# Nine-token runs for k and v, a product in four quarters, and more transposes by transfer, in a two-part attention and MLP kernel

## The chip, the cores and the metric

The kernel runs on one core of a Trainium2 chip. A core has a matrix engine (PE, fed by a stream of weight loads, PEld), three engines for elementwise work (DVE, ACT, POOL), a queue engine (SP) and 16 DMA engines shared by the queues of SP (q1) and POOL (q0). Matrix results go to PSUM, from where DVE and ACT copy them. The metric is the device time of one execution in microseconds (us), as the median of several runs.

## The reference

There are 8 batches of 8 heads, 576 tokens and 64 columns a head. All inputs and the output are float32.

```python
kv = np.einsum('bhsd,bhse->bhde', k, v)
out = np.einsum('bhsd,bhde->bhse', q, kv)
rms = np.sqrt(np.mean(out * out, axis=-1, keepdims=True) + 1e-06)
x = (out / rms * g_norm)            # then laid out as (batch, 576 tokens, 512 columns)
theta = x @ w_theta
zr, zi = x * np.cos(theta), x * np.sin(theta)
y = np.einsum('ts,bsd->btd', w_tok_r, zr) + np.einsum('ts,bsd->btd', w_tok_i, zi)
u = x + y
return u + np.maximum(u @ w_ch, 0.0)
```

## The kernel before

**Work and order.** Each batch is cut into tasks for one engine each. A batch has five token tiles: four of 128 tokens (j = 0 to 3) and a tail of 64. A long table, `TURNS`, gives the order in which all tasks of all batches are issued; a letter behind a number puts a copy on another engine (A for ACT, D for DVE), and `r15` means 15 matmuls on constants that keep PE busy. Each engine works its own instructions in that order and waits, in order, for what they need. So a task's place in the table decides what stands behind it when it waits.

**A batch, in tasks.** `load k`, `load v` (SP) and `load q` (POOL). `kv`: the product of k and v per head on PE (L278, L285), summed over 576 tokens, in float32. `ko`: copies of it into `kbd` (L307 on ACT, L309 on DVE), each head twice, in the upper and the lower 64 partitions. `qt`/`qd`: q turned, by PE in batches 0 and 1, by a transposing transfer afterwards (L330). `raw`: q times kv (L344, L353). `sq`, `ss`, `rt`, `x`: square (ACT), sum (DVE), reciprocal root (POOL, L382), scaled x (DVE, L405). `xt`/`xd`: x turned, by PE (L302, tile `xps`) in batches 0 to 4 and by a transfer (L433, tile `xd`) from batch 5 (`XD`). `xo`: its copy, scaled by g (L257 on ACT, L259 on DVE). `th`: x times w_theta (L464, L467). `pt`, `ar`, `ab`, `si`, `co`, `z`: reduction of the angle, sine, cosine, products with x (ACT and DVE). `y`: the token product on PE (L554), the largest piece of work. `um`: u (DVE, L569). `ut`/`ud`: u turned back, by PE (L302, tile `ups`) or, in batches 5 and 6 (`UD`), by a transfer (L596). `v`: u times w_ch (L464, L467). `fin` and `st`: the last sum (DVE, L612, L617) and the store (SP).

**The weights.** At the start POOL's queue loads the theta weights (`wth`) and the imaginary and real token weights (`toki`, `tokr`), SP's the channel weights, which are scaled once (`wc`, L259 on POOL). PE turns the token weights in nine pieces (`wt`, L642, L643), DVE or ACT copies each into `wT` (`wo`, L307, L309). No y can start before them and before the first z.

**How k and v lie.** In batch 0 a partition holds nine consecutive tokens of a head, and a pair of heads fills 128 partitions. In the other batches 128 partitions hold four tokens each of every head, and the last 64 tokens are a second transfer (L206) into a tile whose lower half is padded with zeros. A head pair there takes ten matmuls of 128 rows by 64 columns, five steps of two heads side by side; the four pairs share one accumulator.

```python
    PS_TR, PS_RAW, PS_ACC = ("tr", 2), ("raw", 2), ("acc", 4)
```

There are four accumulators of the kind `acc`: kv, th, y and v take them in turn, and one is free again when its readers are done.

Of the kernel before, what the change touches and what calls it, by code (L numbers as in the profile page):

```python
# [9 lines left out]
FP32 = mybir.dt.float32  # L10
# [19 lines left out]
0 1 8 4 5 6 7 2 18 3 9 10 11 14 15 r15 31 39 32 47 13 16 17 24 25 33 40 34A 48 23 19 20 35 49 41 36  # L30
55 50 42 51 37 52 38A 12 56D 53 54 21 63 71 57 64D 43 72 58 73 65 74 44 r2 137 133 59 45 75 46 60 66
76 138A 134A 61 62 67 77 68 79 89 125 90D 69 70 126 80 91 107 92 108 81D 78 93 98 82 116 117D 94 99
83 95 118 100 129 127 84 85 119 96 86 101 128 87 130 102 120 97 121 88 109 139 141 171 159 122 110
104 123 140 142A 103 124 111 112 105 28 29 26 22 206 27 207 208 30 201 163 135 131 202 113 136 114
106 132D 115 203 204 155 172 160 161 229 173 164 165 156 215 216 162 174 230 166 167 157 147 148 143
168 169 144 158 170 222 145 185 209 210 211 212 149 151 213 186 223D 214 146 150 152 217 231 236 153
243 218 232 237 244 219 154 220 233 205 388 366 377 187 190 175 234 357 188 221 177 192 224 191 176
178 235 225 250 226 251D 238 259 358 227 239 260D 240 193 353 354 514 355 194 356 189 195 252 180
261 196 253 181 262 228 254 245 360 361 241 255 242 263 264 268 362 363 246 256 257 265 266 364 365
247 269D 258 248 359 249 270 286 277 389 271 390 287D 278 288 182 267 391 272 273 183 279 315 367  # L40
289 274 392 275 290 393 291 276 378 311 280 292 293 281 282 379 283 323 312 319 320 430 316 324 284
368 431 294 501 525 502 536 503 504 179 285 369 317 313 318 314 380 505 370 381 321 307 308 325 303
322 326 371 304 305 309 299 300 432 310 382 403 394 433 306 404D 395D 342 301 372 383 396 373 384
397 302 374 434 435 405 347 197 508 509 510 511 406 348 436 437 385 398 407 399 408 438 198 375 386
441 440 439 506 442 295 296 344 400 343 401 513 512 409 376 387 345 402 412 515 526 297 421 422D 298
413 516 410 414 337 423 332 339 349 517 411 415 338 527 416 417 350 528 418 424 419 507 518 529 653
519 425 426 340 530 656 657 658 659 451 542 520 427 428 660 521 420 661D 522 334 537 459 452 662 523
429 543 538 333 335 524 460 453 471 472 473 551 454 539 540 531 461 455 532 552 474 673 684 346 649
650 184 651 652 533 541 456 467 457 468 469 663 534 462 458 535 470 578 327 553 664 328 554 665 579D
463 674 464 560 666 654 465 580 675 555 561D 466 676 556 557 581 558 667 582 677 562 544 563 583 564  # L50
565 685 447 448 329 490 569 545 584 686 566 567 570 585 491 443 449 444 445 546 559 678 687 450 586
446 330 688 571 690 492 668 689 547 691 572 548 669 341 821 810 336 475 679 477 726 573 568 574 727D
670 493 655 589 590 587 588 801 671 797 331 798 832 799 800 494 804 476 575 680 478 681 699 805 806
807 497 728 495 700 549 809 550 808D 496 576 729 682 701 485 692 498 672 730 577 731 480 599 600 591
811 592 593 702 481 486 683 703 822 717 607 601 812 693 705 704 694 594 602 813 814 732 733 823 696
608 603 609 604 605 595 718D 610 734 815 606 824 719 596 597 708 619 735 825 738 802 720 709 706 598
721 695 707 620 615 616 710 621 611 833 826 711 834 697 612 613 623 617 622 722 835 618 836 736 803
737 837 712 698 713 614 625 628 487 816 827 482 714 624 828 817 715 488 626 829 818 483 716 950 629
723 724 838 479 956 872 943 951 952 953 643 767 819 725 847 644 955 820 954D 763 751 764 752 768 769
765 747 748 830 749 638 957 753 831 766 770 873D 754 750 958 839 959 962 848 630 755 960 484 967 855  # L60
489 627 978 944 849 963 756 757 874 850 851 964 631 840 945 946 875 852 639 841 758 961 876 965 947
739 743 740 744 741 968 745 759 842 877 966 742 856 969 853 878 746 970 864D 879 760 640 973 771 761
# [3 lines left out]
898 899 985 904 908 983 896 993D 977 986 889 890 1096 987 900 988 1097 994 891 885 1098 892 909 1107  # L66
1099 995 1108 1018 1001 632 989 996 1109 1110 786 886 913 887 914 888 1100 997 990 1019 998 991 999
1002 1010D 782 915 910 911 1101 1020 783 916 912 1111 992 352 775 1117 637 199 1003 1118 793 937
1102 1021 1022 1023 784 1011 1004 1024 1103 1005 794 499 780 642 1123 917 796 785 648 1104 1025 1012
1119 918 928 923 1026 1013 1120 1006 1014 1105 1007 787 919 1008 924 929 1000 1132D 788 1015 1030  # L70
# [4 lines left out]
1141D 1139 1150 1142 940 1161 1162 935 1151 1152 1074 1163 1143 1164 1084 1144 1085 1069 1075 1146  # L75
# [27 lines left out]
def kernel(  # L103
# [12 lines left out]
    nc = tc.nc  # L116
    B, H, S, D = q.shape
    C = H * D
    P = 128
# [21 lines left out]
    NX, NXE = 7, 4  # L141
    QD = 2

    XD = 5
    UD = (5, 6)

    ZD = 2
# [750 lines left out]
```

## Time and profile before

| | |
|---|---|
| median of the runs shown | 220.69 us (220.33 to 221.16, 3 runs) |
| the profiled execution's own time | 222.68 us |
| its span, first to last instruction | 220.9 us |
| mean granted clock of PE | 0.973 |
| PE busy | 200.5 us, 91% |
| DVE busy | 175.2 us, 79% |
| ACT busy | 132.2 us, 60% |
| POOL busy | 97.3 us, 44% |
| transfers | 70,059 packets, 43.43 MB, mean 197 GB/s |

Busy time counts an engine that is at work. Matmuls overlap, so an instruction's duration on PE is longer than the distance to the next; the distance is what a row of many equal instructions shows. The chain of work that ended last is followed back from the last instruction, at each step to what released it. A wait is put down to the semaphore that came last.

### The profile page before, as it was taken

How to read it: one execution, taken by the hardware profiler on the slowest of the kernel's cores; microseconds unless marked ns; L12 is line 12 of the kernel's file. 1: busy time of each engine (PE TensorE's matmuls, PEld its weight loads, DVE VectorE, ACT ScalarE, POOL GpSimd, SP SyncE). 2: the span in 40 equal slices, each digit the busy share in tenths (PEclk: the TensorE clock that was granted, in tenths of full speed). 3: DMA queues.
4: the chain of work that ended last, by engine and by line, in shares of the span. 5: the costliest groups of instructions: out<-in, count | busy, mean ns of one | idle time of the engine just before them, and what ended most of it. 6: DMA issues, size and time to landing. Idle time of an engine off the chain costs nothing.

```text
span 220.9 us, 5506 instructions
## 1 busy us (share of the span) xinstructions
PE 200.5 (91%) x2177; PEld 137.7 (62%) x2177; DVE 175.2 (79%) x371; ACT 132.2 (60%) x268; POOL 97.3 (44%) x102
## 2 busy tenths in 40 slices
PE   7398699799799999989999999999999999999991
PEld 2275356596465768757578776866587746756850
DVE  4018649627989989897999988999997999999662
ACT  2028479317499249762788854947865888557050
POOL 8225930002953529556649158435724545204000
PEclk9969769999999999999999999999999999999998
DMA  6999999954999999959999976998980776764374
GB/s 229 274 275 238 236 231 234 271 163 27 260 140 209 297 183 306 122 85 258 307 203 289 137 226 137 240 240 225 163 141 12 225 181 166 178 114 117 110 262 154
DMA packets 70059, 43.43 MB, mean 197 GB/s; under 512 B 39570, under 2 KB 63762, under 8 KB 70034
## 3 DMA queue, kind: packets, MB, share of 16 engines
q1 hardware_dynamic: 55602, 35.73, 64.7%
q0 software_dynamic: 14432, 7.36, 25.0%
q8 instruction: 17, 0.28, 0.5%
q14 instruction: 8, 0.07, 0.1%
HBM read 33.06 MB, written 9.44 MB: 192 GB/s over the span
## 4 chain that ended last, share of the span: by engine, by line
PE 60%; DVE 14%; DMA 9%; POOL 8%; ACT 5%; issue 2%; POOLq 0%; DVEq 0%; ACTq 0%
PE y L554 26%; PE v L464 10%; PE th L464 10%; DMA wth<-in_moe_w_theta_dram 9%; POOL rt L382 5%; PE kv L285 5%; DVE arg L486 2%; DVE ss L375 2%; PE ups L302 2%; PE raw L344 2%; DVE x L405 2%; DVE zm L531 2%; PE th L467 2%; PE xps L302 1%; PE v L467 1%
## 5 line engine op out<-in xcount | busy, mean ns | idle before, releaser
L382 POOL TENSOR_TENSOR rt<-ss,mhalf 128x8 f32<-128x8 f32 (+1 forms) x35 | 54.9, 1572 | 81.7 <-DVE ss L375 81.5
L554 PE MATMUL y<-wT,zm 128*128 128x256 f16 (+1 forms) x512 | 76.0, 286 | 1.9 <-DVE zm L531 1.0
L554 PEld LDWEIGHTS <-zm 128*128 128x128 f16 x512 | 47.7, 98 | 17.2 <-DVE zm L531 2.6
L569 DVE SCALAR_TENSOR_TENSOR wn<-y,gcol,xT 128x256 f16<-128x256 f32 (+2 forms) x72 | 32.6, 478 | 8.2 <-PE y L554 7.7
L464 PE MATMUL th<-wth,xT 128*128 128x512 f16 x128 | 34.2, 395 | 2.0 <-DMA wth<-in_moe_w_theta_dram 1.6
L480 ACT ACTIVATE pt<-th 128x512 f32<-128x512 f32 (+1 forms) x40 | 21.8, 550 | 20.7 <-PE th L464 13.1
L464 PE MATMUL v<-wch,wn 128*128 128x512 f16 x128 | 31.6, 379 | 0.0
L486 DVE SCALAR_TENSOR_TENSOR arg<-pt,th 128x512 f32<-128x512 f32 (+1 forms) x40 | 24.8, 627 | 4.2 <-ACT pt L480 4.0
L509 ACT ACTIVATE sc<-arg,quarter 128x512 f16<-128x512 f32 (+1 forms) x40 | 27.0, 675 | 1.2 <-DVE arg L494 1.1
L502 ACT ACTIVATE sc<-arg 128x512 f16<-128x512 f32 (+1 forms) x40 | 23.4, 587 | 6.9 <-DVE arg L486 6.6
L366 ACT ACTIVATE sqb<-raw 128x512 f32<-128x512 f32 x32 | 18.5, 592 | 14.7 <-PE raw L344 13.4
L405 DVE TENSOR_TENSOR x<-raw,rt 128x512 f16<-128x512 f32 x32 | 21.8, 684 | 3.0 <-POOL rt L382 2.6
L375 DVE TENSOR_REDUCE ss<-sqb 128x8 f32<-128x520 f32 x32 | 21.8, 686 | 2.5 <-ACT sqb L366 2.3
L531 DVE TENSOR_TENSOR zm<-x,sc 128x1024 f16<-128x1024 f16 x32 | 21.7, 682 | 0.5 <-ACT sc L509 0.5
L617 DVE SCALAR_TENSOR_TENSOR us<-v,us 128x512 f32<-128x512 f32 (+1 forms) x32 | 19.4, 616 | 2.0 <-PE v L467 0.8
L307 ACT CAST kbd<-kv 64x256 f16<-64x256 f32 (+1 forms) x28 | 9.4, 334 | 19.1 <-PE kv L278 12.4
L464 PEld LDWEIGHTS <-xT 128*128 128x128 f16 x128 | 11.6, 100 | 13.4 <-issue 3.3
L588 ACT ACTIVATE us<-ups 128x512 f32<-128x512 f16 (+1 forms) x32 | 17.0, 541 | 4.1 <-PE ups L302 2.6
L537 POOL DMA_DIRECT2D zt<-zf x24 | 13.6, 574 | 12.4 <-PE v L467 11.1
L464 PEld LDWEIGHTS <-wn 128*128 128x128 f16 x128 | 11.8, 98 | 11.2 <-issue 0.6
L285 PE MATMUL kv<-vt,kt 128*64 128x64 f32 x560 | 18.3, 223 | 0.0
L554 PE MATMUL y<-wT,zt 128*128 128x320 f16 (+1 forms) x64 | 18.3, 286 | 0.0
(78 smaller groups left out, 249.2 us busy)
## 6 DMA issues: line engine op xcount, KB each, us to landing
kt<-in_k_dram SPq DMA_DIRECT2D x7, 1024.0 KB, 9.1
vt<-in_v_dram SPq DMA_DIRECT2D x7, 1024.0 KB, 8.0
out_dram<-us SPq DMA_DIRECT2D x24, 256.0 KB, 3.4
qh<-in_q_dram POOLq DMA_DIRECT2D x7, 512.0 KB, 11.3
out_dram<-vs SPq DMA_DIRECT2D x8, 256.0 KB, 2.3
zm<-in_moe_w_ch_dram SPq DMA_DIRECT2D x1, 1024.0 KB, 12.0
out_dram<-us SPq DMA_DIRECT2D x16, 64.0 KB, 2.1
kt<-in_k_dram SPq DMA_DIRECT2D x7, 128.0 KB, 7.4
```

The costliest lines, as they stand in the source:

```text
L285: nc.tensor.matmul(t[i * D:(i + 1) * D, hp - lo, :], kt[b % NKV][:, 2 * hp + i, j, :], vt[b % NKV][:, 2 * hp + i, j, :], start=(j == 0), s ...
L375: nc.vector.reduce_sum(out=ss[:], in_=sq_sb.pop((b, j))[:], axis=AXX)
L382: nc.gpsimd.tensor_tensor(out=rt[:], in0=ss[:], in1=mhalf[:, 0:h], op=ALU.pow)
L405: nc.vector.tensor_tensor(out=x_pair[b, p][:, :, a * HC:(a + 1) * HC].rearrange("p t (h e) -> p h t e", e=D), in0=r[:].rearrange("p (h t e ...
L464: nc.tensor.matmul(t[:], lhs(kc), w[:, kc, :], start=first, stop=last)
L480: nc.scalar.activation(out=pt[:], in_=th_ps[b, j][:], func=AFT.Copy, bias=MAGIC)
L486: nc.vector.scalar_tensor_tensor(out=arg[:, 0, :], in0=pt_sb.pop((b, j))[:], scalar=MAGIC, in1=th_ps.pop((b, j))[:], op0=ALU.subtract, op1 ...
L502: nc.scalar.activation(out=sc[:, 0, :], in_=arg_sb[b, j][:, 0, :], func=AFT.Sin, bias=0.0, scale=-TURN * SHRINK,)
L509: nc.scalar.activation(out=sc_sb[b, j][:, 1, :], in_=arg_sb.pop((b, j))[:, 1, :], func=AFT.Sin, bias=quarter[:], scale=-TURN * SHRINK,)
L531: nc.vector.tensor_tensor(out=dst, in0=x.unsqueeze(1).broadcast_to((P, 2, w)), in1=sc[:], op=ALU.mult)
L554: nc.tensor.matmul(t[:, 0:hi - lo], s, wT[:, w, lo:hi], start=n == 0, stop=n == len(z) - 1)
L569: nc.vector.scalar_tensor_tensor(out=dst, in0=y_in, scalar=gcol[:, 0:1], in1=x_in, op0=ALU.mult, op1=ALU.add,)
```

## The change

**k and v** now lie in nine-token runs in every batch: one transfer for k and one for v, without the tails and without the padding. A head pair's even head is in the upper 64 partitions and its odd head in the lower.

**The product** (`kv_quad`, task `kq`) handles four heads at a time: 36 matmuls of 64 rows by 64 columns, in the order upper rows and left columns, lower rows and left columns, upper and right, lower and right. The two row halves write two different accumulators, so a batch holds two; both quads of a batch use the same two, except in batch 0, where each has its own.

**The copies** take one accumulator at a time: eight pieces of 64x128 a batch (sixteen of 64x64 in batch 0), each contiguous in `kbd`, whose heads lie in a new order (`slot`).

**Turning.** x is turned by a transfer from batch 3 on (before: 5), u in batches 4, 5 and 6 (before: 5 and 6).

**Order.** The whole table is new. The diff, with the table cut to its first lines:

```diff
 TURNS = """
-0 1 8 4 5 6 7 2 18 3 9 10 11 14 15 r15 31 39 32 47 13 16 17 24 25 33 40 34A 48 23 19 20 35 49 41 36
...
+0 1 7 8 9 10 13 14 12 2 r11 27 3 30A 5 31A 6 28 19 r2 45 37 4 46 29D 17 38 47 18 39 48 40 49 53 61
...
-    XD = 5
-    UD = (5, 6)
+    XD = 3
+    UD = (4, 5, 6)
...
-    kt = [const.tile([P, H, NT, D], FP32, name=f"kt{i}") for i in range(NKV)]
-    vt = [const.tile([P, H, NT, D], FP32, name=f"vt{i}") for i in range(NKV)]
+    kt = [const.tile([P, NHP, S], FP32, name=f"kt{i}") for i in range(NKV)]
+    vt = [const.tile([P, NHP, S], FP32, name=f"vt{i}") for i in range(NKV)]
...
     def pairs_in(eng, dst, src, b, lo, hi):
         eng.dma_start(
-            out=nines(dst)[:, lo:hi, :],
+            out=dst[:, lo:hi, :],
...
-    def heads_in(eng, dst, src, b, hs):
...
-    def tails_in(eng, dst, src, b, hs):
...
-    def pad(eng, i):
...
+    def kv_quad(b, g, banks):
+        if banks is None:
+            banks = [ps.tile([P, NG, D], FP32, tag="acc", bufs=4, name="kv") for r in range(2)]
+        for j in range(NN):
+            js = slice(j * D, (j + 1) * D)
+            for c in range(2):
+                for r in range(2):
+                    at = slice(r * D, (r + 1) * D)
                     nc.tensor.matmul(
+                        banks[r][c * D:(c + 1) * D, g, :], kt[b % NKV][at, 2 * g + c, js],
+                        vt[b % NKV][at, 2 * g + c, js], start=(j == 0), stop=(j == NN - 1),
                     )
+        for r in range(2):
+            kv_ps[b, g, r] = banks[r]
+
+    def slot(h):
+        return 4 * (h % 2) + 2 * (h // 2 % 2) + h // 4
+
+    def kv_out(b, gs, r, i, eng):
+        at = slice(i * D, (i + 1) * D)
+        lo, n = gs[0], len(gs)
+        for c in range(2):
+            src = kv_ps[b, lo, r][c * D:(c + 1) * D, lo:lo + n, :]
+            first = slot(4 * lo + 2 * c + r)
+            copy_out(eng, kbd[b % 2][at, first:first + n, at], src)
...
-    for a, (lo, hi) in enumerate(((0, NH2), (NH2, NH2 + 1), (NH2 + 1, NHP))):
...
+    for a in range(NG):
+        k_got[0, a] = [add(f"load {x}0{'ab'[a]}", "SP",
+                           lambda a=a, t=t, src=src: pairs_in(nc.sync, t[0], src, 0, 2 * a, 2 * a + 2))
+                       for x, t, src in (("k", kt, k), ("v", vt, v))]
         if not a:
+            add("hold s", "SP", lambda: hold_sync(vt[0][0:1, 0, 0:1]), k_got[0, 0][1:])
...
+        k_ = [add(f"load k{b}n", "SP", lambda: pairs_in(nc.sync, kt[b % NKV], k, b, 0, NHP), old),
+              add(f"load v{b}n", "SP", lambda: pairs_in(nc.sync, vt[b % NKV], v, b, 0, NHP), old)]
```

Three places show how the order moves.

POOL at the start; `wn_86` and `wnt_88` are the imaginary token weights, `wn_85` and `wnt_87` the real ones, `wch` the scaled channel weights, `qh_69` q of batch 1. Before:

```order
L224 DMA wn_86<-in_moe_w_tok_i_dram 128x2304
L229 DMA wnt_88<-in_moe_w_tok_i_dram 64x576
L232 DMA wth<-in_moe_w_theta_dram 128x4x512
L224 DMA wn_85<-in_moe_w_tok_r_dram 128x2304
L229 DMA wnt_87<-in_moe_w_tok_r_dram 64x576
L212 DMA qh_69<-in_q_dram 128x8x256
```

Now:

```order
L209 DMA wn_86<-in_moe_w_tok_i_dram 128x2304
L214 DMA wnt_88<-in_moe_w_tok_i_dram 64x576
L217 DMA wth<-in_moe_w_theta_dram 128x4x512
L240 TENSOR_SCALAR wch<-zm_77 128x512
L209 DMA wn_85<-in_moe_w_tok_r_dram 128x2304
L214 DMA wnt_87<-in_moe_w_tok_r_dram 64x576
L240 TENSOR_SCALAR wch<-zm_77 128x512
L197 DMA qh_69<-in_q_dram 128x8x256
```

Two scalings of the channel weights, which wait for these weights, have moved ahead: one in front of the real token weights, one in front of q of batch 1.

ACT from its first `pt` (L480, now L462) in batch 0 through sine and cosine (L502, L509; now L484, L491); `wT` is a copy of turned token weights, `xT` of turned x. Before:

```order
L480 ACTIVATE pt<-th 128x512
L257 ACTIVATE xT_82<-xps,gcol 128x4x128 x2
L480 ACTIVATE pt<-th 128x512
L502 ACTIVATE sc<-arg 128x512
L480 ACTIVATE pt<-th 128x256
L509 ACTIVATE sc<-arg,quarter 128x512
L502 ACTIVATE sc<-arg 128x512
L480 ACTIVATE pt<-th 128x512
L307 COPY wT<-wps 128x576
L509 ACTIVATE sc<-arg,quarter 128x512
L502 ACTIVATE sc<-arg 128x256
L480 ACTIVATE pt<-th 128x512
```

Now:

```order
L462 ACTIVATE pt<-th 128x512 x2
L484 ACTIVATE sc<-arg 128x512
L491 ACTIVATE sc<-arg,quarter 128x512
L462 ACTIVATE pt<-th 128x512
L484 ACTIVATE sc<-arg 128x512
L491 ACTIVATE sc<-arg,quarter 128x512
L289 COPY wT<-wps 128x576
L462 ACTIVATE pt<-th 128x256
L462 ACTIVATE pt<-th 128x512
```

The two copies of x have left the chain. Of four weight copies between the first pt and the last cosine, one is left; the others are on DVE (before, three more follow the rows shown).

SP around x of batch 3, now turned by transfers (`xd`), between stores (`out`), q of batches 4 and 5 (`qD`) and k, v of batch 5:

```order
L190 DMA kt_65<-in_k_dram 128x4x576
L312 DMA_TRANSPOSE qD<-qe_72 128x2x128
L607 DMA out_dram<-us 128x512
L415 DMA_TRANSPOSE xd<-x 128x8x128
L312 DMA_TRANSPOSE qD<-qh_69 128x8x128
L415 DMA_TRANSPOSE xd<-x 128x2x128
L607 DMA out_dram<-us 128x512 x2
L190 DMA vt_67<-in_v_dram 128x4x576
L415 DMA_TRANSPOSE xd<-x 128x8x128
```

Before, no `xd` stands there; each k and v of batch 5 was a pair of transfers, and nothing of x was ahead of v.

More of the change, by code (lines that the diff above doesn't have):

```diff
@@ L717 @@
         ko = {}
[L718 to L726 removed]
+        first = None
+        for g in range(NG):
+            own = b == 0 or not g
+            t = add(f"kq {b} {g}", "PE",
+                    lambda b=b, g=g: kv_quad(b, g, [kv_ps[b, 0, r] for r in range(2)] if g and b else None),
+                    [*k_got[b, g], None if own else first], [PS_ACC, PS_ACC] if own else [])
+            if own:
+                first = t
+            last["kv", b] = t
+            if b and not g:
+                continue
+            gs = [g] if b == 0 else [0, 1]
+            outs = []
+            for r in range(2):
+                for i in range(2):
+                    outs.append(add(f"ko{len(gs)} {b} {g}{r}{i}", "DVE" if r else "ACT",
+                                    lambda e, b=b, gs=gs, r=r, i=i: kv_out(b, gs, r, i, e),
+                                    [t, *of("raw", b - 2), *(outs[-1:] if i else [])],
+                                    alt=("ACT", "DVE")))
             first.readers = outs
[L728 to L730 removed]
+            ko.update({x: outs for x in gs})
         ko[2] = ko[0] + ko[1]
```

141 lines of the change are left out of this document (34 added, 107 removed), and 32 rows, old and new, of the table TURNS.

## The prediction

> **What bounds the kernel now.** I read the page first, then the busy time in four stretches, then the chain of work that ended last, and only then the rows of the parts that the change touches.
>
> ```profile
> span 220.9 us, 5506 instructions
> ...
> core 0: us, PE busy (x) PEld busy (x) DVE busy (x) ACT busy (x) POOL busy (x), PEclk, DMA share, GB/s
> 0.00:42.00 42.00, 31.29 (x321) 19.81 (x322) 21.18 (x56) 21.11 (x46) 17.89 (x28) 0.88 1.13 247
> 42.00:110.00 68.00, 63.18 (x804) 44.91 (x801) 56.88 (x114) 40.55 (x83) 34.27 (x29) 1.00 0.97 198
> 110.00:210.00 100.00, 99.96 (x1015) 69.73 (x1009) 92.56 (x196) 67.38 (x134) 45.09 (x46) 1.00 0.80 173
> 210.00:220.90 10.90, 6.09 (x50) 3.27 (x48) 4.55 (x9) 3.15 (x6) 0.00 (x0) 0.93 0.58 205
> ```
>
> Three regimes. To 42 us, transfers and then a chain over ACT and DVE keep PE from its main work, and the clock is at 0.88. From 42 to 110, PE (63 of 68) and DVE (57 of 68) alternate. From 110 to 210, PE is without a gap and DVE is 92.6% busy: whatever leaves PE there is worth time only until DVE fills up.
>
> ```profile
> 5.42 20.46 DMA wth<-in_moe_w_theta_dram
> 25.92 1.86 PE th L464 x4
> ...
> 41.35 0.58 PE y L554 x3
> ...
> 137.34 0.45 PE raw L344 x8
> 137.79 0.86 PE v L464 x4
> 138.65 2.52 PE kv L285 x80
> ```
>
> The chain says the same in order: the theta weights land at 25.9, the token product (y) runs steadily only from 41.35, and later PE follows PE. It also gives PE's real prices: 0.86/4 = 215 ns for a 512-column matmul, 0.45/8 = 56 ns for a 128-column one, 2.52 us for the k-v product of a batch.
>
> **The k-v product.** Before, a batch has 40 matmuls of 128 rows by 64 columns (two instructions each in the trace, being fp32), two column halves side by side. Now it has 72 of 64 by 64, four quarters side by side, hence 144 instructions.
>
> ```profile
> L285 PE MATMUL kv<-vt,kt 128*64 128x64 f32 x560 | 18.3, 223 | 0.0
> ...
> 6.21 1.26 PE L278 MATMUL kv<-vt,kt 64*64 64x64 f32 x36
> 47.49 2.55 PE L285 MATMUL kv<-vt,kt 128*64 128x64 f32 x80
> 19.43 0.32 PE L353 MATMUL raw<-kbd,qT 128*64 128x64 f16 x8
> ...
> L353 PE MATMUL raw<-kbd,qT 128*64 128x64 f16 x16 | 0.6, 201 | 0.1
> ```
>
> Without the last instruction's own 0.22 us, 80 in 2.55 are 29.5 ns apart, and 36 of batch 0, which already work in two diagonal quarters, are (1.26-0.22)/35 = 29.7 ns apart. Half the rows make a matmul no quicker, so the spacing is that of two units, each taking one per 59 ns. With four units it would be 14.7 ns: 144 x 14.7 = 2.1 us against 2.36, a gain of 0.2 us a batch. With no overlap of the two row halves it stays at 29.5: 4.25 us, a loss of 1.9 a batch. The two-byte row lets me choose: eight instructions in 0.32 us with 0.20 for the last are (0.32-0.20)/7 = 17 ns apart, so instructions can be issued nearly that densely. I take the gain. The page "TensorE: Matmul & The Clock Gate" of the Trainium skill (section "Wait — 56ns, not 53.3ns?") says that start-to-start never falls below about 25 ns; by it a batch would take an estimated 3.6 us, and the whole forecast would stand near 225 us. The trace's 17 ns speaks against this floor where halves work side by side.
>
> **Copies out of the product.** Four of 64x256 a batch become eight of 64x128, and in batch 0 eight of 64x128 become sixteen of 64x64.
>
> ```profile
> L307 ACT CAST kbd<-kv 64x256 f16<-64x256 f32 x20 | 7.3, 364 | 6.5 <-PE kv L285 6.3
> L309 DVE CAST kbd<-kv 64x256 f16<-64x256 f32 x8 | 3.4, 421 | 3.6 <-ACT kbd L307 3.4
> L307 ACT CAST kbd<-kv 64x128 f16<-64x128 f32 x8 | 2.1, 259 | 12.5 <-PE kv L278 12.4
> L569 DVE SCALAR_TENSOR_TENSOR wn<-y,gcol,xT 128x256 f16<-128x256 f32 x40 | 18.6, 478 | 3.4 <-PE y L554 3.1
> L569 DVE SCALAR_TENSOR_TENSOR wn<-y,gcol,xT 128x320 f16<-128x320 f32 x24 | 12.8, 546 | 4.9 <-PE y L554 4.6
> L569 DVE SCALAR_TENSOR_TENSOR wn<-y,gcol,xT 128x64 f16<-128x64 f32 x8 | 2.2, 275 | 0.0
> L259 DVE TENSOR_SCALAR xT<-xps,gcol 128x512 f16<-128x512 f16 x10 | 4.6, 474 | 0.1
> L259 DVE TENSOR_SCALAR xT<-xd,gcol 128x512 f16<-128x512 f16 x5 | 1.7, 343 | 0.0
> ```
>
> On ACT the half-size copy is 259 against 364 ns. DVE has no such row: it lies between its 64-column piece (275) and the full copy (421); ACT's ratio gives 300. In batches 1 to 7 DVE has 24 such copies instead of 8 large ones: 7.2 - 3.4 = +3.8 us, of which batches 4 to 7 have 14 x 0.30 - 6 x 0.42 = +1.7. ACT goes from 20 x 0.364 to 32 x 0.259, +1.0. The product now holds two of the four accumulators until all eight copies are done, where it held one; y, th and v need the rest. I cost that at nothing, since PE has the other two, and keep 0.3 us a batch (one copy's length) as the upper end.
>
> **x by transfers in batches 3 and 4, u in 4.** PE loses 2 x 18 + 16 = 52 transposes of 56 ns: 2.9 us, all after 110. ACT keeps a copy for each. DVE cuts u's 320-column pieces in two (4 x (0.478 + 0.275 - 0.546) = +0.8 us) and reads x from a cheaper place (343 instead of 474 ns); over batches 3 to 7 its share of these copies changes from 2 full-size from PSUM, 5 from transfers and 3 half-size ones (about 0.3 us each) to 8 full ones from transfers, about -0.9. Six x and four u transfers join SP's queue.
>
> ```profile
> 8.98 7.05 SPq L206 DMA_DIRECT2D kt<-in_k_dram  x1
> 16.08 5.44 SPq L200 DMA_DIRECT2D vt<-in_v_dram  x1
> 157.85 1.28 SPq L433 DMA_TRANSPOSE xd<-x  x1
> 184.14 1.28 SPq L596 DMA_TRANSPOSE ud<-wn  x1
> ...
> SPq L433 <- DVE x L405: 17.7, 3, 8.9
> ...
> xd<-x SPq DMA_TRANSPOSE x9, 3.2
> ud<-wn SPq DMA_TRANSPOSE x8, 2.5
> ```
>
> Each holds SP for about 1.3 us: +13 us on a queue with room for it, while 14 tail loads leave; two of the many-piece loads alone held SP for 12.5 us at the start. SP now also has q's first transfer of batch 2 ahead of k and v of batches 2 and 3; it waits there for q, but these k are not asked for before 60 us: nothing. The wait added is ACT's and DVE's for a landing, 3.2 us after issue, behind whatever SP waits for first (up to 8.9 us for x). Queued behind a waiting transfer are stores and the next k, v; who waits for it is theta of that batch, and then PE. The new order puts x's transfers of batch 3 right behind the producer, well ahead of th, so I cost the wait at nothing; rival four prices the other case.
>
> **The start.** Three things move. SP holds back the second half of k, v until the first v has landed. POOL issues the real token weights only behind its first scaling of the channel weights. ACT does one of the nine weight copies inside the theta chain instead of four, and no x copy there after the first theta.
>
> ```profile
> 27.82 0.60 ACT L480 ACTIVATE pt<-th 128x512 f32<-128x512 f32 x1 [2.65 <-PE th L464]
> 39.85 0.72 ACT L509 ACTIVATE sc<-arg,quarter 128x512 f16<-128x512 f32 x1
> ...
> L307 ACT COPY wT<-wps 128x576 f16<-128x576 f16 x6 | 3.6, 634 | 0.2 <-PE wps L643 0.2
> L257 ACT ACTIVATE xT<-xps,gcol 128x512 f16<-128x512 f16 x10 | 6.7, 685 | 0.8 <-PE xps L302 0.8
> ...
> 6.19 0.62 POOL L224 DMA_DIRECT2D wn<-in_moe_w_tok_r_dram x1
> 19.46 2.97 POOL L259 TENSOR_SCALAR wch<-zm 128x512 f16<-128x512 f32 x2 [1.88 <-DMA zm<-in_moe_w_ch_dram]
> ...
> wn<-in_moe_w_tok_r_dram POOLq DMA_DIRECT2D x1, 576.0 KB, 22.6
> qh<-in_q_dram POOLq DMA_DIRECT2D x7, 512.0 KB, 11.3
> ```
>
> From the first pt (27.82) to the end of the last cosine (40.57) ACT is what y waits for. Leaving that stretch: 3 x 0.634 + 2 x 0.685 = 3.3 us. Against it: the real token weights now land at 6.19+22.6 = 28.8. After the change they are issued after the first scaling, 19.46+1.5+0.6 = 21.6; with the 11.3 us of a similar load on that queue, 32.9. PE asks for them behind five thetas, at 25.9 + 4 x 0.86 + 0.45 = 29.8, and ACT behind seven activations, about 31.3. So between nothing and about 2 us is lost, and 3.3 us is the gain's upper end. I take **-2.0**, bounds -3.3 and +1.
>
> **The sum**, against the profiled execution's own 222.68 us (span 220.9 and 1.8 around it; the median of the runs, 220.69, is 2.0 below). Start: -2.0. Between 42 and 110: PE -0.6 for three products, DVE +2.1 for three batches of copies, in a stretch where DVE has 11 us free: 0, with 3 either way because the order of a chain over five engines is new. From 110: PE could lose 2.9 + 5 x 0.21 = 3.95; DVE gains 1.7 + 0.8 - 0.9 = 1.6 and would stand at 94.2 in 96 us, 98%. It has not shown that over a whole stretch, so I take **-2.5** (94.2 in 97.5, 96.6%), bounds -3.95 and 0. Tail: the same instructions, 0. Together -4.5: 218.2 in a profiled execution, **216.2 us** as a median. With the bounds of each term that are likely together, 214 to 219 for this case.
>
> **The rivals.** A measurement of this kernel tells about 0.5% (1.1 us) from no change: 219.6 to 221.8 is "same".
> 1. *Forecast*, 216.2: chance 0.45.
> 2. *The middle stretch shortens too.* Fewer k, v pieces free SP and the transfers, which are at 0.97 of 16 engines there, and the order closes gaps: the other 3 us and the rest of the late gain, about 212. For it: PE is 5 us idle there. Against: DVE's copies. Chance 0.13.
> 3. *DVE becomes the bound.* The late gain is lost (+2.5) and the middle pays most of its DVE copies (+1.8): 220.5. For it: 92.6 of 100 already. Against: ACT is 67 of 100 and took part of the copies. Chance 0.17.
> 4. *Slower: the quarters do not run four abreast.* At 29.5 ns a batch's product takes 4.25 us, +1.9 x 7 = 13 us, and the credited 0.7 is gone: 230. Three of the batches lie where PE is 4.8 us idle; with half of that as cover, 227. It outweighs the gains once a batch's 144 instructions take more than 2.36 + (4.5+0.7)/7 = 3.1 us. For it: no row shows more than two units at once. Against: the 17 ns row, and separate accumulators for the two row halves, on which nothing in the trace bears. The page "TensorEngine Tiling (Array Packing)" of the Trainium skill (section "Gotcha 1: PSUM Pressure") says that row tiles cannot use one PSUM bank at the same time; the change keeps to that, and no run here shows what a breach costs. Chance 0.14.
> 5. *The new order waits somewhere*: the token weights stall ACT's whole chain at the start, or SP's queue holds x of batch 3 or 4 (one 8.9 us wait at that place). +6 us on the forecast: 222.5. Chance 0.11.
>
> **Chances.** Faster by over 0.5%: cases 1 and 2, 0.58. Within 0.5%: 0.17. Slower by over 0.5%: cases 4 and 5, 0.25. The range leaves out about half of case 2 and most of case 4: 211.0 to 225.5.
>
> **What would show it.** Right: the block of 144 instructions in 2.1 to 2.5 us; y steady by about 39.5 us; DVE at 95 to 97% in the PE-bound stretch; ten more transfers with PE still without gaps. Wrong: the block near 3.6 or 4.2 us; ACT waiting for the real token weights; PE waiting for x behind a transfer in batches 3 and 4; DVE at 99% with PE waiting for z or for accumulators.

## The result, and the profile after

The changed kernel takes 233.0 us (median of 4 runs, 230.6 to 233.8) against 220.9 (4 runs, 220.3 to 221.5) of the kernel before on the same chip: a ratio of 1.053, 95% interval 1.045 to 1.061. That is 12 us slower, above the upper end of the range. Some of the kernels below show two speeds up to 3% apart; ratios compare undisturbed runs with undisturbed runs, so a median and a ratio can differ by a per cent.

The page of the changed kernel, and its busy time in the stretches that the prediction used:

```profile
span 232.0 us, 6323 instructions
PE 197.2 (85%) x2574; PEld 134.3 (58%) x2574; DVE 181.1 (78%) x398; ACT 133.3 (57%) x279; POOL 96.2 (41%) x100
q8 instruction: 20, 0.33, 0.6%
...
core 0: us, PE busy (x) PEld busy (x) DVE busy (x) ACT busy (x) POOL busy (x), PEclk, DMA share, GB/s
0.00:42.00 42.00, 27.42 (x299) 16.58 (x300) 21.77 (x57) 17.20 (x40) 19.70 (x29) 0.81 1.15 244
42.00:110.00 68.00, 59.69 (x1018) 43.90 (x1016) 55.12 (x121) 37.95 (x82) 29.56 (x26) 0.97 0.87 195
110.00:210.00 100.00, 93.48 (x1134) 62.82 (x1132) 91.55 (x200) 71.23 (x146) 44.83 (x41) 1.00 0.83 181
```

Where PE had no gap before (99.96 of 100 us), it now idles 6.5 us, and between 42 and 110 us another 3.5 more than before. DVE is not fuller: 91.55 of 100 against 92.56.

PE's granted clock fell too, which the prediction did not price: to a mean of 0.81 before 42 us (0.88 before the change) and 0.97 from there to 110 (1.00). Between 100 and 110 us it was 0.83, behind the longest stall shown below; the first row is from before the change, the second from after.

```profile
100.00:110.00 10.00, 9.62 (x89) 6.39 (x87) 9.03 (x19) 5.18 (x10) 6.31 (x6) 1.00 1.18 292
100.00:110.00 10.00, 8.71 (x72) 6.58 (x73) 6.52 (x16) 3.86 (x9) 3.21 (x2) 0.83 0.53 112
```

By these means 68 us at 0.97 lose an estimated 2 us of PE's work. No run changed the clock alone.

One row of the groups splits the loss: the first and last start of the token product y, before and after.

```profile
L554 PE MATMUL y<-wT,zm x512: 270/290/311, 36.5 to 209.8; 128*128 128x256 f16 x86, 128*128 128x320 f16 x85
L536 PE MATMUL y<-wT,zm x512: 270/297/474, 41.4 to 221.3; 128*128 128x256 f16 x88, 128*128 128x320 f16 x83
```

The start lost 4.9 us (36.5 to 41.4), the body from first y to last 6.6 (173.3 to 179.9); the tail is the same. The timeline of PE, product rows alone, shows where part of it went; the bracket is the idle time before the row and what ended it, and x counts matmul instructions, 144 a batch.

```profile
6.27 1.28 PE L261 MATMUL kv<-vt,kt 64*64 64x64 f32 x72 [0.24 <-DMA vt<-in_v_dram]
19.63 2.20 PE L261 MATMUL kv<-vt,kt 64*64 64x64 f32 x72 [8.36 <-DMA vt<-in_v_dram]
...
47.39 2.20 PE L261 MATMUL kv<-vt,kt 64*64 64x64 f32 x134
50.76 0.44 PE L261 MATMUL kv<-vt,kt 64*64 64x64 f32 x10 [1.17 <-issue]
...
94.97 2.31 PE L261 MATMUL kv<-vt,kt 64*64 64x64 f32 x141
101.29 0.47 PE L261 MATMUL kv<-vt,kt 64*64 64x64 f32 x3 [4.01 <-issue]
...
145.85 2.33 PE L261 MATMUL kv<-vt,kt 64*64 64x64 f32 x144 [0.69 <-issue]
```

The quarters do run four abreast: (1.28 - 0.22)/71 and (2.33 - 0.22)/143 are 15 ns. But in batch 4 PE does 141 of 144, then waits 4.0 us for nothing that the profile knows ("issue"), then does the last three. The waits sum up the same:

```profile
PE kv L261 <- DMA vt<-in_v_dram: 8.6, 2, 8.4
PE kv L261 <- issue: 6.7, 5, 4.0
...
ACT xT L238 <- DMA xd<-x: 5.9, 5, 1.8
PE y L536 <- DMA zt<-zf: 2.0, 3, 1.4
```

So the first suspicions were: A, the dense product outruns the loading of its own instructions; B, the held-back second half of k and v of batch 0 costs the start; C, the transfers of x and u come late.

### The profile page after: what moved, and what is told of

The parts are those of the page before. It is cut to its first block, busy times and chain, and to the rows that moved or that the text cites. A ratio compares the mean times of both kernels' runs of the same rounds, so it can differ in the third digit from the quotient of the medians.

```text
span 232.0 us, 6323 instructions
## 1 busy us (share of the span) xinstructions
PE 197.2 (85%) x2574; PEld 134.3 (58%) x2574; DVE 181.1 (78%) x398; ACT 133.3 (57%) x279; POOL 96.2 (41%) x100
## 5 line engine op out<-in xcount | busy, mean ns | idle before, releaser
L364 POOL TENSOR_TENSOR rt<-ss,mhalf 128x8 f32<-128x8 f32 (+1 forms) x35 | 55.5, 1588 | 69.6 <-DVE ss L357 69.4
L536 PE MATMUL y<-wT,zm 128*128 128x256 f16 (+1 forms) x512 | 77.4, 290 | 1.5 <-DVE zm L513 1.0
L536 PEld LDWEIGHTS <-zm 128*128 128x128 f16 x512 | 48.8, 99 | 17.5 <-DVE zm L513 2.3
L261 PE MATMUL kv<-vt,kt 64*64 64x64 f32 x1152 | 21.9, 226 | 15.9 <-DMA vt<-in_v_dram 8.6
L446 PE MATMUL th<-wth,xT 128*128 128x512 f16 x128 | 32.6, 385 | 2.3 <-ACT xT L238 1.5
L462 ACT ACTIVATE pt<-th 128x512 f32<-128x512 f32 (+1 forms) x40 | 21.9, 552 | 16.4 <-PE th L446 10.6
L261 PEld LDWEIGHTS kv<-vt,kt 64*64 64x64 f32 x1152 | 19.8, 140 | 19.5 <-issue 16.2
L491 ACT ACTIVATE sc<-arg,quarter 128x512 f16<-128x512 f32 (+1 forms) x40 | 26.9, 675 | 0.6 <-DVE arg L476 0.5
L484 ACT ACTIVATE sc<-arg 128x512 f16<-128x512 f32 (+1 forms) x40 | 23.4, 587 | 4.2 <-DVE arg L468 4.1
L289 ACT CAST kbd<-kv 64x128 f16<-64x128 f32 (+1 forms) x42 | 10.4, 247 | 25.8 <-PE kv L261 25.0
L519 POOL DMA_DIRECT2D zt<-zf x24 | 12.8, 540 | 23.9 <-PE v L446 17.7
L570 ACT ACTIVATE us<-ups 128x512 f32<-128x512 f16 (+1 forms) x28 | 14.6, 533 | 13.0 <-PE ups L284 11.2
L291 DVE CAST kbd<-kv 64x128 f16<-64x128 f32 (+1 forms) x30 | 8.2, 274 | 16.2 <-PE kv L261 15.8
```

Of the source, the lines that this page charges most:

```text
L261: nc.tensor.matmul(banks[r][c * D:(c + 1) * D, g, :], kt[b % NKV][at, 2 * g + c, js], vt[b % NKV][at, 2 * g + c, js], start=(j == 0), stop ...
L364: nc.gpsimd.tensor_tensor(out=rt[:], in0=ss[:], in1=mhalf[:, 0:h], op=ALU.pow)
L446: nc.tensor.matmul(t[:], lhs(kc), w[:, kc, :], start=first, stop=last)
L462: nc.scalar.activation(out=pt[:], in_=th_ps[b, j][:], func=AFT.Copy, bias=MAGIC)
L484: nc.scalar.activation(out=sc[:, 0, :], in_=arg_sb[b, j][:, 0, :], func=AFT.Sin, bias=0.0, scale=-TURN * SHRINK,)
L491: nc.scalar.activation(out=sc_sb[b, j][:, 1, :], in_=arg_sb.pop((b, j))[:, 1, :], func=AFT.Sin, bias=quarter[:], scale=-TURN * SHRINK,)
```

## The experiments

**B alone: the hold.** The loads k0b and v0b go ahead of the transfer that holds SP until the first v has landed.

```diff
 SP: load k0a, load v0a,
-hold s, load g0, load k0b, load v0b, load wch
+load k0b, load v0b, hold s, load g0, load wch
```

> The changed kernel, but the second half of k and v of batch 0 is issued at once, ahead of the transfer that waits for the first v. Theory B (start): the 8.4 us that PE stands waiting for that v shrinks to 2 us or less and the first y starts 3 to 5 us earlier (36-38 instead of 41.4): 228-230. Theory A says nothing of the start: there the token and theta weights end the wait anyway, they land later by what k and v take from them, and the time stays within 2 us, 231-235.

Measured: ratio 1.033 (1.028 to 1.038), against 1.053 with the hold. The row of y:

```profile
L536 PE MATMUL y<-wT,zm x512: 270/290/474, 36.2 to 215.4; 128*128 128x256 f16 x88, 128*128 128x320 f16 x83
```

The first y is back where it was before the change (36.2), the body is as long as in the changed kernel (179.2). The hold costs some 4 us (2.0% by the ratios); theory B holds.

**A: the number of sums.** The changed kernel with five of the nine token runs of each product (four are left out): 80 instructions a batch, here called sums, as many as before the change, but each a quarter.

```diff
-        for j in range(NN):          # nine token runs of each quarter
+        for j in range(5):
```

> The changed kernel, but the k-v product sums only the first five of the nine token runs (160 PE instructions a batch instead of 288 with their weight loads); order, transfers and copies as they are. Theory A (PE runs through the dense block faster than its instructions are loaded): the stalls marked 'issue' inside the product, about 8.6 us in batches 1 to 7, go almost wholly, and with the 0.9 us less of work a batch the time falls by 8 to 12 us, to 221-225. Theory B (the loss is the new order and its late transfers): only the work itself goes, 0.9 us a batch at most, half of it hidden: 228-231.

Measured: 228.0 us, ratio 1.030 (1.021 to 1.039). Its instruction loads on the page, PE's longest wait on y, and the row of y:

```profile
q8 instruction: 16, 0.26, 0.5%
...
PE y L536 <- DMA zt<-zf: 7.5, 4, 4.3
...
L536 PE MATMUL y<-wT,zm x512: 270/297/471, 40.2 to 215.3; 128*128 128x256 f16 x88, 128*128 128x320 f16 x83
```

PE has no wait on issue in the product any more, and the body shrinks to 175.1 us, 4.8 less; by the pitch, 64 sums of 15 ns less in each of seven batches would be 6.7, and 6.7 of waits on issue are gone as well. Part of that went into a wait of 4.3 us for the transfers of zt of batch 2, which the stall in batch 4's product had covered. Theory A is right on the waits and missed the time: 228.0 us, where it expected 221 to 225.

**A: the pace.** The same 144 sums and instructions, one row half after the other, so that only two run side by side.

```diff
-        for j in range(NN):
-            for c in range(2):
-                for r in range(2):
+        for r in range(2):
+            for j in range(NN):
+                for c in range(2):
```

> The changed kernel with the two row halves of the product one after the other instead of in turn: the same 144 sums a batch, the same number of instructions, but only two run side by side (29.5 ns from one to the next as in the kernel before, 4.25 us a batch instead of 2.1). Theory A (the block of four abreast runs through its instructions faster than they are loaded, 6.7 us of waits on issue): the sums themselves cost up to 15 us more in the seven batches, but most of the waits on issue in the product are gone, so the blocks of batches 1 to 7 last some 30 us together instead of 23 and the whole is 233 to 241, less than 7 us longer. Rival A' (the loads of instructions are late whatever the pace, because queues full of other transfers hold them): the waits on issue stay at 5 us or more and the time is 243 to 250.

Measured: 232.9 us, ratio 1.054 (1.046 to 1.063), the same as the changed kernel. Its product in the timeline (batches 4 and 6), and two of PE's waits:

```profile
96.43 3.83 PE L261 MATMUL kv<-vt,kt 64*64 64x64 f32 x141
101.16 0.33 PE L261 MATMUL kv<-vt,kt 64*64 64x64 f32 x3 [0.90 <-issue]
...
144.41 3.90 PE L261 MATMUL kv<-vt,kt 64*64 64x64 f32 x144
...
PE y L536 <- DMA zt<-zf: 3.8, 3, 1.9
PE kv L261 <- issue: 0.9, 1, 0.9
```

Spaced at 26 ns, the product waits 0.9 us on issue instead of 6.7. A block of 3.9 us costs the kernel nothing against one of 2.3: running four abreast bought no time here.

That these waits are for code, the traces show directly: they hold the time of every load of instructions (queue q8, 16,384 bytes each). In batch 4 (us):

| run | product begins | PE stops | load of code | PE goes on |
|---|---|---|---|---|
| changed kernel | 94.97 | 97.28 | 98.70 to 99.81 | 101.29 |
| two abreast | 96.43 | 100.26 | 98.78 to 99.80 | 101.16 |
| loads later (under D) | 88.77 | 91.09 | 89.42 to 90.64 | 92.14 |

Every wait on issue of 0.4 us or more inside a product, in all runs of this document that have one, ends 1.2 to 1.7 us behind the end of such a load. Some waits of that name are something else: the 0.69 us ahead of batch 6's product in the changed kernel has no such load near it. A holds as to the stalls.

**A: parts.** With the early loads, each product cut in six parts of 24 sums with other PE work between them.

```diff
-kv_quad(b, g, banks)                  # j in range(NN)
+kv_quad(b, g, banks, lo, lo + 3)      # lo = 0, 3, 6, each a step of its own in the order
```

> The changed kernel with the loads of the second halves of k and v of batch 0 issued ahead of the hold (as in the run of that edit alone, 231.1 us), and with each product block of batches 1 to 7 cut in six parts of 24 sums with other TensorE work between them. Same sums, same instructions, same pitch inside a part. Theory A: the code is asked for at a lower pace, the waits on issue in the product fall below 2.5 us in sum (7.8 with the loads alone), and the time to 223 to 228. Rival (the loads of instructions are only held by data on the queues, or the wait covers another): waits on issue stay above 5 us, or as much is waited for the transfers of zt, and the time stays at 229 to 233.

Measured: ratio 1.080 (1.070 to 1.091), slower than all before it; waits on issue of PE at the product still 5.9 us, of which 3.2 are for code and 2.7 stand ahead of batch 6's product with no load of code near. My expectation, under 2.5 us of waits and a faster kernel, failed. Two accumulators are now held over six parts, and other work had to move behind the product; which of the two cost more was not separated.

**C: the transfers.** First in the new order, with x of batches 3 and 4 and u of batch 4 turned on PE again; then in the order before, x by transfers from batch 3 and u in 4 to 6, each transfer of x right behind the x that it turns.

```diff
-    XD = 3, UD = (4, 5, 6)     (the new order)
+    XD = 5, UD = (5, 6)
 
-    XD = 5, UD = (5, 6)        (the kernel before)
+    XD = 3, UD = (4, 5, 6)
```

> The changed kernel with the turns of x in batches 3 and 4 and of u in batch 4 back on TensorE, as before the change, in the new order; product and loads as changed. Theory C (the transfers cost 3 to 4 us of waits late, against 2.9 us that TensorE saves): between 230 and 233, the waits for xT of batch 3 gone, those on issue in the product the same. Rival (transfers are the main cost): under 229. Rival (transfers gain what was predicted, 2.9 us, and the waits would be there anyway): 235 to 237.

> The kernel before with the other part of the change: x turned by transfers from batch 3, u in 4 to 6; order, k, v and the product as before. Theory A: no part in the loss; PE loses 2.9 us of transposes and gives some of it back in waits for the transfers: 218-222. Theory C (the transfers come late and PE waits for x): 224-228.

Measured: 239.3 us, ratio 1.084 (1.075 to 1.094), and 247.5 us, ratio 1.120 (1.115 to 1.124). In the new order the transfers, all ten together, save about 6 us, so C falls there; no theory expected more than 237. In the old one they cost 26, where 3 to 7 were expected: PE waits for x behind SP's queue, as the waits of the second kernel show:

```profile
DVE xT L259 <- DMA xd<-x: 11.3, 3, 5.6
ACT xT L257 <- DMA xd<-x: 10.6, 3, 5.9
...
PE th L464 <- DVE xT L259: 5.3, 2, 5.2
```

**D: what stands in front of the code.** In the stretch of the 4 us stall, 84 to 103 us, the changed kernel's DMA queues (packets, MB, share of 16 engines) and issues (KB each, us to landing) are

```profile
q1 hardware_dynamic: 4536, 3.01, 77.0%
q0 software_dynamic: 1979, 0.75, 32.1%
q8 instruction: 3, 0.05, 1.1%
...
kt<-in_k_dram SPq DMA_DIRECT2D x1, 1152.0 KB, 6.5
qh<-in_q_dram POOLq DMA_DIRECT2D x1, 512.0 KB, 10.6
zt<-zf POOLq DMA_DIRECT2D x4, 32.0 KB, 6.7
```

The DMA engines have no room left (77.0% and 32.1%), three instruction loads stand among 6,500 packets of data, and k of batch 5 and q of batch 6 are issued just ahead. So the next run keeps the early loads and holds k and v of batch 2 until product 1 is copied out, and k of batch 5 and q of batch 6 until after product 4.

```diff
+def hold_kbd(b): nc.sync.dma_start(out=gate_h[:], in_=kbd[b % 2][0:1, 0, 0:1])
 SP:   load k2n, load v2n behind hold 1;  load k5n behind hold 4
 POOL: load q6 behind zv 2 10
```

> The changed kernel with the early loads of batch 0 (231.1 us alone), and with two groups of large loads held back until the product before which they were queued is done: k and v of batch 2 (2.3 MB) behind the copies of product 1, and k of batch 5 and q of batch 6 (1.7 MB) behind product 4 and the transfers of zt of batch 2. Theory D (the product's instructions and the transfers of zt stand in the DMA queues behind these loads; it is not the pace of the product alone): the stalls of 3.1 us in product 1 and of 4.0 us in product 4 fall to under 1.5 us each, and no wait for zt of batch 2 takes their place; 223 to 227 us. Theory A alone (the pace of the four abreast outruns the loading of instructions whatever else is under way): both stalls stay within 1 us and the time within 229 to 233.

Measured: ratio 1.029 (1.019 to 1.039), 228.9 us. Two rows of PE's timeline:

```profile
92.14 0.33 PE L266 MATMUL kv<-vt,kt 64*64 64x64 f32 x3 [1.05 <-issue]
...
102.96 1.46 PE L451 MATMUL th<-wth,xT 128*128 128x512 f16 x3 [3.96 <-DVE xT L245]
```

Batch 4's stall falls from 4.0 us (3.8 with the early loads alone) to 1.05. The table above says why: its load of code starts 0.65 us after the product begins instead of 3.7, and between 88.8 and 89.4 us the DMA engines moved one packet, where in the changed kernel, from 94.97 to 98.6 us, the two data queues took 72.8% and 42.0% of them. The queued data made it long. In sum the waits on issue fall less, from 7.8 us with the early loads to 5.9: batch 2's rises from 0.6 to 1.7, and 2.8 us stand ahead of batch 6's product, with no load of code near. The time hardly moves, since PE then waits 4.0 us for x of batch 3, which now lies behind k of batch 5. With 80 sums as well:

> The same with five of the nine sums of each product (80 a batch, as many as before the change; the other four are left out). Theory D: with 80 sums there was no wait on issue, but one of 4.6 us for zt of batch 2; that wait is gone, so 219 to 223. Theory A alone: 224 to 228, with the wait for zt still above 3 us.

Measured: 228.5 us, ratio 1.024 (1.016 to 1.032), not clearly better than with 80 sums alone and above the 219 to 223 that D expected; 2.7 us of wait on issue stand ahead of batch 6's product here too. Then all loads that had stood in front of a wait were moved: k of batch 5 behind the first transfer of x of batch 3, v of batch 5 behind the second, k of batch 3 behind product 2, v of batch 6 next to k of batch 6; once with all sums, once with 80.

> The run with two groups of loads held back (228.9 us), with three more moved: k of batch 5 behind the first transfer of x of batch 3 instead of right ahead of it (x was waited for 4.1 us there), v of batch 5 behind the second, k of batch 3 behind product 2 (1.9 us of wait on issue in it), v of batch 6 right behind k of batch 6 instead of just ahead of product 6 (3.2 us of wait on issue there). All 144 sums. Theory D (the loads stand in the way): the three waits fall under 1.5 us each, 219 to 224 us. Rival (something else takes the place each time; the new order is bound there by another chain): 226 to 230.

> The same with five of the nine sums of each product (80 a batch; the others are left out). If the extra instructions cost little once the loads are out of the way: within 3 us of the run with all sums (by the pitch alone 64 sums of 14.9 ns are 1 us a batch, 7 us in sum, less what lies beside other waits). If they are what is left of the loss: 5 to 8 us less than it.

Measured: 1.049 (1.042 to 1.056) and 1.037 (1.030 to 1.044). Both expectations failed. In the first of the two the largest of PE's waits are

```profile
PE qps L289 <- DMA qh<-in_q_dram: 3.3, 2, 2.9
PE y L541 <- DMA zt<-zf: 3.3, 2, 2.8
PE raw L331 <- DMA qD<-qh: 2.6, 2, 2.0
PE kv L266 <- DMA vt<-in_v_dram: 2.5, 1, 2.5
```

where the wait on issue, now 1.2 us in sum, used to be first. D explains the long stalls inside the product, but in these runs moving loads only changed who waits.

**Which part of the change costs in the old order.** The order and the turns of before, with the loads in nine-token runs, the quarters and the copies (products moved back where the second accumulator is not free yet); then the same with 80 sums.

```diff
 (order and XD, UD of the kernel before; loads, product, copies of the changed one)
-kv b 0, 1, 2, 3; ko4 b 0, 1
+kq b 0, 1; ko2 b 100, 101, 110, 111      second run: for j in range(5)
```

> The kernel before with one part of the change: k and v in nine-token runs, the product in four quarters and its copies; order and transfers as before, apart from tasks put later where the second accumulator is not free yet. Theory A: the product stalls in any order, so 5 to 9 us over the kernel before, 226-230, with 'issue' waits inside the product. Theory B: the product runs in 2.1 us a batch without stalls; 218-222.

> The order, the turns of x and the turns of u of the kernel before, with the loads in nine-token runs, the quarters and their copies (233.3 us with all sums), and five of the nine sums of each product (80 a batch; the others are left out). If the extra instructions of the product carry the 12 us there: 221 to 225. If the two accumulators held at once, the copies, or the loads in larger pieces carry them: 228 to 233.

Measured: ratios 1.055 (1.050 to 1.060) and 1.024 (1.018 to 1.030). The quarters with their loads and copies alone make the old order as slow as the whole change. Without 64 sums a batch it is 3.1% faster, some 7 us, about their own time by the pitch (6.7). That is no loss against the kernel before, whose 80 sums last longer (2.55 us) than 144 do now (2.33). In the second run PE waits before y for the copies that free the product's accumulators; this is the first of three such rows:

```profile
144.71 1.90 PE L536 MATMUL y<-wT,zm 128*128 128x256 f16 x14 [1.21 <-ACT kbd L289]
```

So accumulators and copies were put into the kernel before by themselves, with its own 80 sums and loads. Its order is kept but for the products of batches 3 and 7 and one piece of y of batch 0, which move back to where two accumulators are free:

```diff
+ if b and hp == lo: kv_ps[b, lo] = t = [t, ps.tile([P, n, D], FP32, tag="acc", bufs=4, name="kv")]
- t[i * D:(i + 1) * D, hp - lo, :], kt[b % NKV]...
+ t[i][i * D:(i + 1) * D, hp - lo, :], kt[b % NKV]...
  second run:
+ for m in range(0, n, 2): copy_out(eng, dst[:, m:m + 2, k_, :], src[:, m:m + 2, :])
```

> The kernel before with the product of batches 1 to 7 in two accumulators held at once (one for each half of the columns) instead of one; the same 80 sums, four copies a batch of the same size. If the second accumulator costs (y waits 1.2 us for ScalarE's copies of kbd in three batches of the run with the old order and 80 sums): 223 to 226. If not: 220 to 222, and the cost lies in the copies or the loads.

> The same, and each of the four copies a batch cut in two of half the size, as many as in the changed kernel. 28 copies of 364 ns become 56 of 259 ns, 4.3 us more on ScalarE and VectorE, and the accumulators are held 0.3 us longer. If the copies cost by the time for which they hold the accumulators: 1.5 to 3 us above the run with two accumulators. If they are beside the path: within 1 us of it.

Measured: 1.028 (1.021 to 1.035) and 1.030 (1.024 to 1.035). The second accumulator, with the moves that it needs, costs 6 us; twice as many copies add nothing that can be told from it. In the first of the two, the busy time from 110 us, PE's rows around the products of batches 6 and 7, one of its waits, and the row of y are

```profile
110.00:210.00 100.00, 94.92 (x955) 65.10 (x953) 87.38 (x185) 64.73 (x128) 44.42 (x45) 1.00 0.72 162
...
141.26 1.90 PE L556 MATMUL y<-wT,zm 128*128 128x256 f16 x14 [1.08 <-DVE kbd L311]
166.16 1.63 PE L556 MATMUL y<-wT,zm 128*128 128x256 f16 x12 [1.20 <-ACT kbd L309]
169.26 0.45 PE L556 MATMUL y<-wT,zm 128*128 128x320 f16 x2 [1.48 <-DVE zm L533]
...
PE kv L287 <- DVE us L619: 1.2, 3, 0.5
...
L556 PE MATMUL y<-wT,zm x512: 269/290/310, 33.2 to 213.3; 128*128 128x256 f16 x86, 128*128 128x320 f16 x85
```

PE, without a gap before, is 5 us idle from 110 to 210. In the rows shown y waits 2.3 us for copies, one of them behind batch 6's product, which was not moved, and 1.5 for z. The product itself, which never waited for an accumulator before, now waits 1.2 us for DVE's readers of v. The body lasts 180.1 us, against 173.3 before; as y happens to start 3.3 us earlier in this profile, the span is 3.4 longer (224.3).

What the quarters and their loads add to that in the old order (1.030 to 1.055) was not separated. The rows of y with eight copies and with the quarters are

```profile
L558 PE MATMUL y<-wT,zm x512: 269/290/310, 35.5 to 216.5; 128*128 128x256 f16 x86, 128*128 128x320 f16 x85
L536 PE MATMUL y<-wT,zm x512: 269/290/310, 39.1 to 221.1; 128*128 128x256 f16 x86, 128*128 128x320 f16 x85
```

The body is 1.0 us longer, with 2.3 us of waits on issue in the product; the other 3.6 are a later first y. Starts that no edit touches lie up to 3 us apart, though (33.2, 35.5 and 36.5 in the three kernels with the loads of before), so this split is not shown.

**DVE and zt late, and one part taken over alone.** With the early loads: all copies of kbd in batches 1 to 7 on ACT (24 copies, two in each of twelve tasks; the expectation counts half); or the last row block of z written by DVE in all batches (ZD = 8) instead of by transfers from batch 2. And the kernel before with u of batch 4 turned by transfers too, as the only edit.

```diff
 (changed kernel)  -ko2 b 1ri on DVE in twelve places   +on ACT
 (changed kernel)  -ZD = 2                              +ZD = 8
 (kernel before)   -UD = (5, 6)                         +UD = (4, 5, 6)
```

> The changed kernel with the early loads of batch 0 (231.1 us alone), and the twelve copies of kbd in batches 1 to 7 that were VectorE's (283 ns each in the middle, 3.4 us in sum) done by ScalarE, 259 ns each. If VectorE sets the pace in the middle and late: 226 to 229. If it does not: 230 to 233, or up to 1 us later where ScalarE copies later than VectorE did and the sums of the next y wait for the accumulators.

> The changed kernel with the early loads of batch 0, and the last row block of z written by VectorE in place in all batches (four operations of 285 ns) as it is in batches 0 and 1, instead of one of 418 ns and four transfers in batches 2 to 7: 24 transfers less, 4.3 us more of VectorE. If the wait for zt is what TensorE loses late: its waits for the transfers of zt (3.0 us in the profile with the early loads) are gone and the time is 227 to 230. If VectorE sets the pace: 233 to 236.

> The kernel before with one part of the change: u of batch 4 turned by transfers too. TensorE loses 16 turns there, 0.9 us at 56 ns each, in the stretch where it hardly waits, so 219.5 to 221 if the transfers stay out of its way. If they hold up SP's queue (the outputs, the turned q of the later batches), as x by transfers did in this order: 222 to 226.

Measured: 1.062 (1.056 to 1.069), 1.049 (1.043 to 1.056) and 1.008 (1.004 to 1.012). With the early loads alone it was 1.033. Relieving DVE of these copies made the kernel slower, so their place on DVE did not set the pace; how much they lost in ACT's queue was not separated. The run without the transfers of zt also gives DVE 4.3 us more work and is some 3.5 us slower, so it does not show what the transfers cost, nor that DVE is free everywhere. The transfers of u in batch 4 lose 0.8% in the old order. And all three suspicions at once (early loads, six parts, turns on PE):

> All three at once: the early loads of batch 0, the product in six parts a batch, and the turns of x in batches 3 and 4 and of u in batch 4 on TensorE. If A, B and C are the whole of the 12 us: 219 to 224, the first y at about 36.5 us as before the change. If something else in the new order or in the copies costs: 225 or more.

Measured: ratio 1.106 (1.095 to 1.117); two of its three edits were harmful alone. No version beat the kernel before.

## Why the prediction was wrong, step by step

- **The product.** The pitch was right: 15 ns against 14.7 worked out. The rule that was weighed there, a floor of 25 ns between starts ("TensorE: Matmul & The Clock Gate" of the Trainium skill), does not hold for four quarters side by side. The block without stalls was as forecast too: 2.33 us against 2.55. What failed is that "a gain of 0.2 us a batch", 1.4 in seven, was taken for the kernel's: it left out that 80 instructions had become 144, whose code must be loaded. PE waited 6.7 us in the products, some 6 of it for code, and at half the pace the kernel took the same time. Rival four named the right place for a wrong reason.
- **The accumulators.** "I cost that at nothing" is the worst step. The kernel before with this edit, and the moves that it needs, is 6 us slower, on average 0.9 us a batch, three times the upper end of 0.3. That end was one copy's length; the rows show y's next accumulator waiting for the copies at their place in ACT's and DVE's queues (1.1 to 1.2 us) and the product waiting for readers of v. They add up to less than 6 us; the rest is not assigned. The page "TensorEngine Tiling (Array Packing)" of the Trainium skill says in "Gotcha 1: PSUM Pressure" that row tiles write to different PSUM banks; these runs give the price of holding a second accumulator here, measured with column halves. Twice as many copies cost nothing more.
- **The start.** "-2.0" was +4.9. I followed ACT's chain behind theta and the token weights (PE waits 1.5 us at most for a weight copy), and passed over the hold, which the text names first of three. With it the second half of the product waits 8.4 us for v; without it, y starts at 36.2, as before the change, so the gain of 2.0 did not come either. Why not was not separated.
- **Transfers.** Cost at nothing against 2.9 us of PE: in the new order right in sign, and larger (about 6). They pay there only, not in the old order. (Where the prediction says that rival four prices a late x, it is rival five.)
- **42 to 110 and later.** "0 with 3 either way" and "-2.5" assumed that only DVE limits. DVE stayed at 91.6%. PE got 6.5 us of gaps after 110 from waits on issue, zt, the turned x and u that stand behind one another, so rival three (DVE) is not what happened, and what rival five says in general, "the new order waits somewhere", is. Of the two places it gave, the token weights held ACT 1.6 us at most; the turned x kept ACT waiting 5.9 us in sum and PE's theta 1.5.

The account closes only in part. In the old order the second accumulator costs 2.8%, the copies nothing more, and the quarters with their loads bring it to 5.5% by a part that is not separated. In the new order, at 5.3%, the hold loses some 4 us and the transfers win some 6. What the second accumulator costs there, in an order that was laid out around it, and what the rest of that order gives was not tried alone, and prices from two orders cannot be added.

## What to carry over

Price a faster instruction mix by three things besides its time on the engine: how many instructions it needs and what is queued ahead of their loading, how many accumulators it holds until which copy, and who is behind that copy. If one wait is taken away and another of the same size appears in the next profile, as here, single moves of loads may not pay; test each part of the change alone in the old order first, and ask of a leaner test whether it removes the work itself or only what was added to it. An edit that seems to pay in one order need not in another.

## What the runs showed of the hardware

Four quarters of a matmul run 15 ns apart, two with 64 rows each 26 ns. With 512 matmuls and 512 weight loads fewer, the page shows 16 instruction loads instead of 20, each of 16,384 bytes in the trace, so some 256 instructions come with one load, and a batch's product of 288 needs more than one in 2.1 us. The page "Runtime: NRT & Kernel Launch" of the Trainium skill says in "Terms" that an engine's instruction memory is refilled in blocks of 16 KiB; the trace agrees with that size. PE goes on 1.2 to 1.7 us behind the end of the load that it waits for. That such a load stands behind data in the same DMA engines is inferred, from the load that started 3.7 us after its product began among full queues and 0.65 us after it with the engines idle; when a load is asked for is not in the trace. Twenty loads are 0.6% of the transfers' time, and waits for them cost PE some 6 us.
